# HGRN2 attention and a MetaFormer MLP on one core: the first MLP product by 15 block products for 18, with the attention moved by half a unit

## The chip, the cores and the metric

The kernel runs on one core of a Trainium2 chip. A core has a matrix engine (TensorE, PE in the profile, with its weight loads as PEld), VectorE (DVE), ScalarE (ACT), GpSimd (POOL), and queues that issue DMAs (SP above all). The metric is the device time of one execution in microseconds, the median of several runs. About 1% is what a measurement of this kernel can tell from no change.

## What is computed

A gated linear attention over 4 batches, 8 heads, 768 steps and 48 channels, then layer normalisation and a two-layer MLP with a residual. The reference, cut to what matters:

```python
f = 1.0 / (1.0 + np.exp(-f_logit))
for t in range(S):                       # S = 768, state is 48 x 48 for each batch and head
    state = f[:, :, t, :, None] * state + np.einsum('bhd,bhe->bhde', k[:, :, t], v[:, :, t])
    y[:, :, t] = np.einsum('bhd,bhde->bhe', q[:, :, t], state)
x = y.transpose(0, 2, 1, 3).reshape(B, S, H * D)          # 4 x 768 x 384
xn = (x - mu) / np.sqrt(var + 1e-06) * g_ln
out = x + np.maximum(xn @ w_ch1, 0.0) @ w_ch2             # w_ch1 384 x 1536, w_ch2 1536 x 384
```

Both weight matrices arrive as 64-bit floats; all else is 32-bit.

## The kernel before

**Units.** The 768 steps are cut into 12 units of 64 steps. A unit holds the 64 steps of all four batches, so 256 rows of x, as two groups (g) of 128 rows. For each unit runs an attention and an MLP.

**Attention of unit n**, in named steps: `gates` (transposes of f on TensorE, tile tr, then a sigmoid on ScalarE), `after` and `upto` (running products of the gates by a scan on VectorE, 128 x 1040), `kx` and `k` (transposes of k, then kh = k times after, on VectorE), `q` (transposes of q, qh = q times upto), `kept` (the state scaled), `carried` (the state's share of the result, into py), `scores` (kh by qh, into ps), `causal` (the mask, on VectorE, into sc), `kt` (transposes of kh, tile kp), `values` (sc by v, into py; ScalarE copies it to x), `chunk` (the unit's own state, into pn), `state` (state = kept + pn), `stats` and `norm` (mean and variance, 1/sqrt on POOL, xn on VectorE), `turn` (transposes of xn, tile xp, and on ScalarE the multiplication with the gain, into xt). carried, scores, values and chunk are small products on quarters of the matrix engine, 64 x 64 and 64 x 48.

**MLP of unit n** (`mlp`, a generator: each `yield` ends a step). The first product makes h, 1536 x 256, held transposed as 12 blocks of 128 rows: for each block three matmuls of a 128 x 128 piece of w1 against 256 columns of xt are summed in a PSUM bank (tile ph, line 778), and ScalarE applies the ReLU for two blocks at once (line 780). That is six steps. In blocks of 128 rows of x by 128 of its columns, and 128 by 512 pieces of w1, it is 2 x 3 x 3 = 18 block products. The second product runs from unit 2 on by seven products for eight (tiles pp, line 805; in order p1, p2, p6, p5, p7, p3, p4), from four sums of blocks of h on VectorE (`sums`, tiles s1, s2, s4 and one written over h) and four of w2 (`mix`, tiles mixed1 to mixed4). VectorE and POOL add the results up in p1, p1x, u2x, u4x, u4y, and DMAs write them out. Units 0 and 1 use plain products (tile po, line 786).

**PSUM.** A pool of four single banks (`one_bank`), handed out in turn to tr, kp, xp, ph, po and pp, and a pool of two double banks for py, ps and pn. A tile of the first pool can be written when the fourth tile before it has been read.

**What sets the order.** No scheduler does: two tables of tokens, START for units 0 to 2 and UNIT for each later one, are read from left to right, and each token records the instructions of one step on all engines at once. `a5.norm` is the step norm of unit 5's attention, `m4` the next step of unit 4's MLP, `l6f` the load of f for unit 6, `s4` the sums of unit 4, `f`, `r` and `w` fetch a piece of the weights and turn it into 32 bits, `t` is one third of mix, `d` an idle product that has no use for the result. Each engine takes its instructions in that order. In UNIT before, with m the unit whose MLP runs, all steps of attention n = m + 1 stand between the thirteen steps of MLP m:

```python
a{n}.gates m{m} a{n}.after m{m} m{m} a{n}.upto a{n}.kx a{n}.k m{m} a{n}.q a{n}.kept m{m}
a{n}.kt a{n}.carried a{n}.scores l{o}f l{o}k m{m} a{n}.causal l{o}q s{m} m{m} m{m} a{n}.values
```

Of the kernel before, what the change touches and what calls it, by code (L numbers as in the profile page):

```python
# [302 lines left out]


START = """
l0k f a0.gates a0.kx a0.after l0q l0v l0x d a0.upto f l1f
r d a0.kept a0.k d l1x a0.q l1k a0.carried f l1q a0.scores
a0.causal w a0.kt a0.values a0.stats r w a1.gates a0.norm a0.chunk a0.state a1.after
f a0.turn f a1.upto a1.kx l1v f f f r r m0
a1.k w a1.kept m0 l2k f a1.q f a1.carried a1.kt r a1.scores  # L310
w a1.causal a1.values r l2v r w l2f a1.chunk a1.stats m0 w
m0 f a1.norm r m0 w f a1.turn r w m0 w
r a1.state m1 m1 m1 m1 w l3v r m0 a2.gates m1
m0 r w a2.after l2q m1 w a2.kx a2.k t l3k m0
m0 l2x m0 a2.upto a2.q a2.kept l3q m0 a2.carried a2.scores m1 m1
a2.causal m1 m1 a2.kt a2.values a2.stats a2.norm a2.chunk l3f a2.state m1 m1
a2.turn l4v a3.gates t m2 a3.kx a3.after a3.k m2 a3.upto a3.kept a3.q
m2 a3.carried a3.scores l4k m2 l4q a3.kt l4x m2 m2 l3x l4f
a3.causal s2 a3.values a3.chunk a3.state t m2 m2 a3.stats m2 m2 m2
a3.norm m2 a3.turn m2  # L320
"""
UNIT = """
a{n}.gates m{m} a{n}.after m{m} m{m} a{n}.upto a{n}.kx a{n}.k m{m} a{n}.q a{n}.kept m{m}
a{n}.kt a{n}.carried a{n}.scores l{o}f l{o}k m{m} a{n}.causal l{o}q s{m} m{m} m{m} a{n}.values
a{n}.chunk m{m} a{n}.stats m{m} m{m} l{o}v a{n}.norm m{m} l{o}x a{n}.turn a{n}.state m{m}
"""


# [1 line left out]
def kernel(  # L330
# [19 lines left out]
    nc = tc.nc  # L350
    B, H, S, D = q.shape
    P = 128
    T = 64
    G = B // 2
# [5 lines left out]
    F = moe_w_ch1.shape[1]  # L360
    KD = DM // P
    KF = F // P
    NU = S // T
    W = B * T
    EPS = 1e-6
    LEAST = 1e-12
    PLAIN = 2
    PIECE = 768

    outer = ctx.enter_context(tc.tile_pool(name="outer", bufs=1))  # L370
    ident = outer.tile([P, P], FP32)
    w1 = outer.tile([P, KD, F], FP32)
# [4 lines left out]
    fast = ExitStack()  # L377
    fast.enter_context(tc.manual_schedule())
    consts = fast.enter_context(tc.tile_pool(name="consts", bufs=1))
    raws = fast.enter_context(tc.tile_pool(name="raws", bufs=2))  # L380
    stage = fast.enter_context(tc.tile_pool(name="stage", bufs=2))
# [3 lines left out]
    ps1 = fast.enter_context(tc.tile_pool(name="ps1", bufs=4, space=PSUM))  # L385

    def two_banks(name):
# [152 lines left out]

    pairs = [(g, a) for g in range(G) for a in range(NP)]
    x_of, norm_of, xt_of, h_of, sums_of = {}, {}, {}, {}, {}

    def half(i):
        return slice(64 * i, 64 * i + 64)
# [195 lines left out]
    def turn(n):  # L743
# [8 lines left out]
                              mul=gain[:, m:m + 1])  # L752
        xt_of[n] = xt

    def sums(n):
# [6 lines left out]
        nc.vector.tensor_tensor(out=s1, in0=a21, in1=a22, op=ALU.add)  # L762
        nc.vector.tensor_tensor(out=s2, in0=s1, in1=a11, op=ALU.subtract)
        nc.vector.tensor_tensor(out=a21, in0=a11, in1=a21, op=ALU.subtract)
        nc.vector.tensor_tensor(out=s4, in0=a12, in1=s2, op=ALU.subtract)
        sums_of[n] = s1, s2, a21, s4

    def mlp(n):

        x = x_of.pop(n)  # L770
        xt = xt_of.pop(n)
        h = work.tile([P, KF, W], FP32, tag="h", bufs=2, name=f"h{n}")
        h_of[n] = h
        for i in range(0, KF, 2):
            ph = one_bank(f"ph{n}").rearrange("p (i t) -> p i t", i=2)
            for j in range(2):
                for m in range(KD):
                    nc.tensor.matmul(ph[:, j], lhsT=w1[:, m, (i + j) * P:(i + j + 1) * P],  # L778
                                     rhs=xt[:, m], start=m == 0, stop=m == KD - 1)
            nc.scalar.activation(out=h[:, i:i + 2], in_=ph, func=AF.Relu)  # L780
            yield
        if n < PLAIN:
            for g in range(G):
                po = one_bank(f"po{n}")[:, 0:DM]
                for i in range(KF):
                    nc.tensor.matmul(po, lhsT=h[:, i, g * P:(g + 1) * P], rhs=w2[:, i],  # L786
                                     start=i == 0, stop=i == KF - 1)
# [12 lines left out]
        t1, t2, t3, t4 = mixed  # L800

        def product(name, a, b):
            pp = one_bank(f"p{name}_{n}")[:, 0:CH]
            for i in range(KH):
                nc.tensor.matmul(pp, lhsT=a[:, i], rhs=b[:, i], start=i == 0, stop=i == KH - 1)  # L805
            return pp


        p1, p1x, u2x, u4x, u4y = [xs.tile([P, CH], FP32, tag=name, bufs=1, name=f"{name}_{n}")
                                  for name in ("p1", "p1x", "u2x", "u4x", "u4y")]  # L810

        def add(engine, to, x1, x2, op=ALU.add):
            engine.tensor_tensor(out=to, in0=x1, in1=x2, op=op)  # L813
# [6 lines left out]
        nc.scalar.copy(out=p1, in_=product("p1", a11, b11))  # L820
# [24 lines left out]
        yield  # L845
# [2 lines left out]

    running = {}

    def run(plan):
        for token in plan.split():
            kind, rest = token[0], token[1:]
            if kind == "a":
                n, stage = rest.split(".")
                if int(n) >= NU:
                    continue
                if "a" + n not in running:  # L860
                    running["a" + n] = attention(int(n))
                running["a" + n].pop(stage)()
            elif kind == "m":
                if token not in running:
                    running[token] = mlp(int(rest))
                next(running[token])
            elif kind == "l":
                load(int(rest[:-1]), rest[-1])
            elif kind == "s":
                sums(int(rest))  # L870
            else:
                {"r": read, "w": write, "f": fetch, "t": mix, "d": idle,
                 "T": lambda: mix(nc.gpsimd)}[token]()

    run(START)
    assert not (queue or fetched or opened)
    for m in range(3, NU):
        run(UNIT.format(m=m, n=m + 1, o=m + 2))
        if m == NU - 2:
            worst = consts.tile([P, 1], FP32)  # L880
            nc.vector.tensor_reduce(out=worst, in_=least, axis=mybir.AxisListType.X, op=ALU.min)
# [4 lines left out]
                                    op=ALU.min)  # L886
            nc.vector.tensor_scalar(out=small, in0=least_one, scalar1=LEAST, scalar2=None,
                                    op0=ALU.is_lt)
    fast.close()

    too_small = nc.values_load(small[0:1, 0:1], min_val=0, max_val=1)
# [33 lines left out]
```

## Time and profile before

| | us |
|---|---|
| median of three runs | 487.04 (486.35 to 490.55) |
| the profiled execution | 489.21 |
| its span | 487.5 |
| TensorE busy in it | 466.0 |
| VectorE busy | 258.1 |
| ScalarE busy | 123.1 |
| POOL busy | 61.8 |

The profiled execution is 2.2 us slower than the median, and its span is 1.7 us shorter than its own time. A group's row gives line, engine, operation, out<-in, shapes and count, then busy time and the mean ns of one, then the idle time ahead of it and what ended it. A row of the chain or of the timeline gives start, length, engine and line. Matmuls in float32 are two instructions each; a transpose is one.

### The profile page before, as it was taken

How to read it: one execution, taken by the hardware profiler on the slowest of the kernel's cores; microseconds unless marked ns; L12 is line 12 of the kernel's file. 1: busy time of each engine (PE TensorE's matmuls, PEld its weight loads, DVE VectorE, ACT ScalarE, POOL GpSimd, SP SyncE). 2: the span in 40 equal slices, each digit the busy share in tenths (PEclk: the TensorE clock that was granted, in tenths of full speed). 3: DMA queues.
4: the chain of work that ended last, by engine and by line, in shares of the span. 5: the costliest groups of instructions: out<-in, count | busy, mean ns of one | idle time of the engine just before them, and what ended most of it. 6: DMA issues, size and time to landing. Idle time of an engine off the chain costs nothing.

```text
span 487.5 us, 11965 instructions
## 1 busy us (share of the span) xinstructions
PE 466.0 (96%) x5207; PEld 417.9 (86%) x5207; DVE 258.1 (53%) x388; ACT 123.1 (25%) x253; POOL 61.8 (13%) x90
## 2 busy tenths in 40 slices
PE   5588999999999999999999999999999999999994
PEld 4467886668899999899899899899899899899894
DVE  6799958328175356356355445544644554544031
ACT  3347732013203213212212212222122222222110
POOL 3225431000020020011011002002002002002010
PEclk9998999999999999999999999999999999999999
DMA  9898982324502303503502602512512521200001
GB/s 169 156 249 221 239 202 50 66 50 91 89 11 57 67 10 75 99 11 70 100 11 57 114 11 56 103 21 53 98 27 45 97 40 27 57 3 22 12 9 32
DMA packets 125964, 36.26 MB, mean 74 GB/s; under 512 B 116432, under 2 KB 122064, under 8 KB 125904
## 3 DMA queue, kind: packets, MB, share of 16 engines
q1 hardware_dynamic: 124128, 35.02, 35.1%
q8 instruction: 43, 0.70, 0.6%
q10 hardware_dynamic: 1776, 0.40, 0.4%
q14 instruction: 17, 0.14, 0.1%
HBM read 30.67 MB, written 4.72 MB: 73 GB/s over the span
## 4 chain that ended last, share of the span: by engine, by line
PE 91%; DVE 3%; SPq 3%; DMA 1%; issue 0%; ACT 0%
PE ph L778 38%; PE pp L805 28%; PE po L786 6%; PE tr L568 5%; PE py L686 3%; PE py L646 2%; PE ps L660 2%; SPq L421 2%; PE pn L716 2%; PE kp L676 2%; PE xp L749 1%; DMA w_256words<-in_moe_w_ch_dram 1%; SPq L411 1%; DVE upto L588 0%; DVE xn L739 0%; DVE after L576 0%
## 5 line engine op out<-in xcount | busy, mean ns | idle before, releaser
L778 PE MATMUL ph<-xt,w 128*128 128x256 f32 x864 | 195.5, 381 | 0.0
L778 PEld LDWEIGHTS ph<-xt,w 128*128 128x128 f32 x864 | 161.4, 191 | 21.5 <-ACT xt L751 0.3
L780 ACT ACTIVATE h<-ph 128x512 f32<-128x512 f32 x72 | 42.9, 597 | 168.9 <-PE ph L778 168.9
L805 PE MATMUL pp<-mixed,h 128*128 128x192 f32 x240 | 42.3, 326 | 0.0
L813 POOL TENSOR_TENSOR p1x<-p,x 128x192 f32<-128x192 f32 x10 | 6.3, 631 | 278.2 <-ACT p L820 278.2
L805 PE MATMUL pp<-mixed,s 128*128 128x192 f32 x240 | 41.5, 329 | 0.0
L805 PE MATMUL pp<-w,h 128*128 128x192 f32 x240 | 40.7, 326 | 0.0
L751 ACT ACTIVATE xt<-xp,gain 128x128 f32<-128x128 f32 x72 | 19.9, 376 | 81.5 <-PE xp L749 81.5
L805 PEld LDWEIGHTS pp<-w,h 128*128 128x128 f32 x240 | 39.5, 190 | 0.5
L805 PEld LDWEIGHTS pp<-mixed,s 128*128 128x128 f32 x240 | 38.8, 190 | 0.4
L805 PEld LDWEIGHTS pp<-mixed,h 128*128 128x128 f32 x240 | 39.1, 190 | 0.0
L576 DVE TENSOR_TENSOR_SCAN after<-gates,ends 128x1040 f32<-128x1040 f32 (+1 forms) x13 | 29.3, 2256 | 13.3 <-ACT gates L605 13.3
L664 DVE TENSOR_TENSOR sc<-ps,causal 128x1024 f32<-128x1024 f32 x12 | 14.7, 1224 | 34.1 <-PE ps L660 34.1
L786 PE MATMUL po<-w,h 128*128 128x384 f32 x96 | 32.2, 488 | 0.0
L762 DVE TENSOR_TENSOR s<-h 128x768 f32<-128x768 f32 x10 | 9.6, 958 | 41.2 <-ACT h L780 41.2
L588 DVE TENSOR_TENSOR_SCAN upto<-gates,starts 128x1040 f32<-128x1040 f32 (+1 forms) x13 | 28.1, 2158 | 0.4
L786 PEld LDWEIGHTS po<-w,h 128*128 128x128 f32 x96 | 17.9, 190 | 11.4
L595 DVE TENSOR_TENSOR kh<-tr,after 128x512 f32<-128x512 f32 x24 | 15.4, 683 | 20.6 <-PE tr L568 20.5
L595 DVE TENSOR_TENSOR qh<-tr,upto 128x512 f32<-128x512 f32 x24 | 15.5, 684 | 19.6 <-PE tr L568 19.6
L568 PE MATMUL tr<-ident,fraw 128*128 128x128 f32 x96 | 14.5, 298 | 9.7 <-DMA fraw<-in_f_logit_dram 9.7
L813 DVE TENSOR_TENSOR u2x<-u2x,pp 128x192 f32<-128x192 f32 x20 | 7.1, 354 | 30.7 <-PE pp L805 30.7
L813 DVE TENSOR_TENSOR p<-p,pp 128x192 f32<-128x192 f32 x20 | 7.1, 353 | 30.1 <-PE pp L805 28.6
(112 smaller groups left out, 542.8 us busy)
## 6 DMA issues: line engine op xcount, KB each, us to landing
w_0words<-in_moe_w_ch_dram SPq DMA_DIRECT2D x7, 768.0 KB, 5.3
kraw<-in_k_dram SPq DMA_DIRECT2D x48, 96.0 KB, 3.0
qraw<-in_q_dram SPq DMA_DIRECT2D x48, 96.0 KB, 3.0
v<-in_v_dram SPq DMA_DIRECT2D x48, 96.0 KB, 3.1
fraw<-in_f_logit_dram SPq DMA_DIRECT2D x46, 96.0 KB, 3.0
vx<-in_v_dram SPq DMA_DIRECT2D x48, 48.0 KB, 2.5
out_dram<-p1x SPq DMA_DIRECT2D x19, 48.0 KB, 2.5
out_dram<-u4y SPq DMA_DIRECT2D x19, 48.0 KB, 2.0
```

The costliest lines, as they stand in the source:

```text
L568: nc.tensor.transpose(pt[:, a * P:(a + 1) * P], src[:, g, 2 * a:2 * a + 2].rearrange("p h e -> p (h e)"), ident)
L576: nc.vector.tensor_tensor_scan(out=at["after"].rearrange(flat)[:, c0:c1][:, ::-1], data0=gt[:, c0 + 1:c1 + 1][:, ::-1], data1=ends.rearran ...
L588: nc.vector.tensor_tensor_scan(out=at["upto"].rearrange(flat)[:, c0:c1], data0=gt[:, c0:c1], data1=starts.rearrange(flat)[:, c0:c1], initi ...
L595: nc.vector.tensor_tensor(out=dst[:, segs], in0=pt, in1=by[:, segs, 1:E1], op=ALU.mult)
L664: nc.vector.tensor_tensor(out=new("sc", [P, 2, GA, T]).rearrange("s r e t -> s (r e) t"), in0=at["ps"].rearrange("s r e t -> s (r e) t"), ...
L686: nc.tensor.matmul(py[half(b), r, e * D:(e + 1) * D], lhsT=sc[rows, r, e], rhs=vx[rows, g, a] if r else vt[rows, g, 2 * a], start=n == 0 a ...
L751: nc.scalar.mul(out=xt[:, m, g * P:(g + 1) * P], in_=pt[:, m], mul=gain[:, m:m + 1])
L778: nc.tensor.matmul(ph[:, j], lhsT=w1[:, m, (i + j) * P:(i + j + 1) * P], rhs=xt[:, m], start=m == 0, stop=m == KD - 1)
L780: nc.scalar.activation(out=h[:, i:i + 2], in_=ph, func=AF.Relu)
L786: nc.tensor.matmul(po, lhsT=h[:, i, g * P:(g + 1) * P], rhs=w2[:, i], start=i == 0, stop=i == KF - 1)
L805: nc.tensor.matmul(pp, lhsT=a[:, i], rhs=b[:, i], start=i == 0, stop=i == KH - 1)
L813: engine.tensor_tensor(out=to, in0=x1, in1=x2, op=op)
```

## The change

From unit 3 on the first product is made by 15 block products (`by_blocks`), each of 128 rows of x by 128, or a sum of such blocks, against a 128 x 512 piece of w1, or a sum of such pieces. A product is four matmuls of 128 columns into one PSUM bank. The sums of blocks of x are made for each unit on VectorE (`sums_of_x`, tile y, 128 x 12 x 128), nine instructions. The sums of pieces of w1 (v0 to v13, 128 x 512 each) are made once, in START, by `mix_first`, one instruction at each token `U` (on POOL, twelve) or `u` (on VectorE, one); they take the memory in which the weights were converted.

Five tiles of a bank each (bw, bx, bv, by, bz) are used in a unit. The first product into a bank overwrites it, and a later product adds to what stands there: bx holds the sum of up to six products. After each product the running sum is read: ScalarE copies it to a block of h (the first time) or VectorE adds it to that block or subtracts it, and ScalarE's ReLU follows when a block is complete. The next product into the same bank comes behind that reading.

The tables of the order are written anew. In UNIT the step q of the next attention, kept, kx, k, kt, upto, after and the gates of the one behind it stand in the unit ahead of where they stood, carried and scores follow the third block product, values the fifth, and chunk the last; turn stands between the second product's first two steps. An MLP has 22 steps for 13, and START holds 11 idle products for 3.

The diff, cut to its core:

```diff
 UNIT = """
-a{n}.gates m{m} a{n}.after m{m} m{m} a{n}.upto a{n}.kx a{n}.k m{m} a{n}.q a{n}.kept m{m}
...
+m{m} m{m} m{m} a{n}.carried a{o}.after a{n}.scores a{n}.causal m{m} m{m} a{n}.values m{m} m{m}
...
+    FIRST = 3
...
+    CW = F // 3
+    late = {}
+    def mix_first():
+        changing.close()
+        pool = changing.enter_context(tc.tile_pool(name="late", bufs=1))
...
+        for to, x1, x2, op in ((v[13], b[1, 3], b[2, 3], add), (v[1], v[13], b[1, 2], sub),
...
+            engine = yield
+            engine.tensor_tensor(out=to, in0=x1, in1=x2, op=op)
...
+    def sums_of_x(n):
+        xt = xt_of[n]
+        a = {(g + 1, k + 1): xt[:, k, g * P:(g + 1) * P] for g in range(G) for k in range(KD)}
+        y = late["pool"].tile([P, 12, P], FP32, tag="y", name=f"y{n}")
...
+                (nc.vector, wide[:, 4 * P:6 * P], flat[:, W:2 * W], flat[:, 0:W], sub),
...
+            engine.tensor_tensor(out=to, in0=x1, in1=x2, op=op)
...
+    def by_blocks(n, h):
+        a, y = y_of.pop(n)
+        v, b = late["v"], late["b"]
+        KB = CW // P
...
+        def product(bank, left, right):
+            new = bank not in banks
+            if new:
+                banks[bank] = one_bank(f"{bank}_{n}").rearrange("p (i t) -> p i t", t=P)
+            for i in range(KB):
+                nc.tensor.matmul(banks[bank][:, i], lhsT=right[:, i * P:(i + 1) * P], rhs=left,
+                                 start=new and i == 0, stop=True, skip_group_check=True)
+            return banks[bank]
+        def copy(to, bank, scale=1.0):
+            nc.scalar.activation(out=out[to], in_=bank, func=AF.Copy, scale=scale)
+        def add(to, bank, op=ALU.add):
+            nc.vector.tensor_tensor(out=out[to], in0=out[to], in1=bank, op=op)
+        def relu(to, bank=None):
+            nc.scalar.activation(out=out[to], in_=out[to] if bank is None else bank, func=AF.Relu)
+        copy((1, 3), product("bw", y[12], b[2, 3]))
+        yield
+        copy((2, 3), product("bx", y[11], v[11]))
+        yield
+        copy((1, 1), product("bv", y[3], b[2, 1]))
+        yield
+        add((1, 3), product("bx", y[9], b[3, 3]))
+        yield
+        add((1, 1), product("by", y[4], b[1, 1]))
+        yield
+        add((1, 1), product("bx", a[1, 3], v[7]), ALU.subtract)
+        relu((1, 1))
+        yield
+        add((1, 3), product("by", a[1, 1], v[13]), ALU.subtract)
+        relu((1, 3))
+        yield
+        copy((1, 2), product("bx", y[10], v[10]))
+        yield
+        add((1, 2), product("by", y[1], v[1]), ALU.subtract)
+        yield
+        copy((2, 2), product("bz", a[2, 2], v[0]), -1.0)
+        yield
+        add((2, 2), product("bx", y[2], b[3, 2]), ALU.subtract)
+        yield
+        add((2, 2), product("by", y[14], b[1, 2]))
+        relu((2, 2))
+        yield
+        add((1, 2), product("bz", y[6], b[2, 2]))
+        relu((1, 2))
+        yield
+        relu((2, 1), product("bx", y[8], v[8]))
+        yield
+        bank = product("by", y[5], v[5])
+        nc.vector.tensor_tensor(out=out[2, 3], in0=bank, in1=out[2, 3], op=ALU.subtract)
+        relu((2, 3))
+        yield
...
-        for i in range(0, KF, 2):
...
+        if n < FIRST:
+            for i in range(0, KF, 2):
...
+        else:
+            yield from by_blocks(n, h)
```

The fifteen products are numbered 1 to 15 in this order; add 6 is the reading of product 6 by VectorE, copy 8 that of product 8 by ScalarE.

More of the change, by code (lines that the diff above doesn't have):

```diff
@@ L305 @@
 START = """
[L306 to L320, printed above, removed]
+l0k f l0q a0.gates l0x a0.after l0v f r a0.kx a0.upto l1f
+d a0.kept a0.k d l1x d d a0.q l1k a0.carried d a0.scores
+d a0.causal a0.values w d r a0.kt a0.stats f l1q d a1.gates
@@ new lines @@
+f l1v a0.chunk d w a0.norm a1.after a0.state a0.turn d a1.upto a1.kx
+a1.k d f r w m0 a1.kept m0 a1.q f f r
+w a1.carried a1.kt r f r l2k f a1.scores a1.causal f l2v
+w l2f f a1.values r a1.chunk f a1.stats m0 m0 r w
+a1.norm m0 a1.turn r w r w a1.state m0 m1 m1 m1
+w m1 w a2.gates r m0 m1 m0 a2.after r l2x w
+l2q w a2.kx a2.k a2.upto m1 m0 a2.q m0 m0 l3q l3k
+a2.kept l3v m0 a2.carried a2.scores U m1 a2.causal a2.values m1 a2.stats a2.norm
+m1 m1 U l3f a2.kt U m1 a2.turn m1 a3.gates T a2.chunk
@@ L321 @@
+m2 a3.after a2.state a3.kx l3x l4f m2 a3.k a3.upto a3.kept m2 a3.q
+U m2 U l4q a3.carried a3.scores a3.kt U U a3.causal U l4x
+a4.gates l4k a3.values T l4v U U a3.chunk m2 a3.stats a3.state t
+l5v U a3.norm m2 s2 a4.after m2 l5f a3.turn m2 m2 a4.kx
+a4.k a4.upto l5x l5k m2 U u m2 a4.q m2 y3 l5q
+a5.gates a4.kt m2 l6f a4.kept
 """
 UNIT = """
-a{n}.gates m{m} a{n}.after m{m} m{m} a{n}.upto a{n}.kx a{n}.k m{m} a{n}.q a{n}.kept m{m}
-a{n}.kt a{n}.carried a{n}.scores l{o}f l{o}k m{m} a{n}.causal l{o}q s{m} m{m} m{m} a{n}.values
@@ L325 @@
-a{n}.chunk m{m} a{n}.stats m{m} m{m} l{o}v a{n}.norm m{m} l{o}x a{n}.turn a{n}.state m{m}
+m{m} m{m} m{m} a{n}.carried a{o}.after a{n}.scores a{n}.causal m{m} m{m} a{n}.values m{m} m{m}
+m{m} m{m} a{n}.stats m{m} m{m} m{m} a{n}.norm m{m} m{m} m{m} s{m} a{n}.chunk
+m{m} a{n}.turn m{m} a{o}.upto a{p}.gates a{o}.kx l{p}v a{o}.k a{n}.state m{m} m{m} m{m}
+a{o}.kt y{n} m{m} a{o}.q l{p}q l{p}x a{o}.kept l{p}k m{m} l{z}f
 """
@@ L385 @@
     ps1 = fast.enter_context(tc.tile_pool(name="ps1", bufs=4, space=PSUM))
+    changing = ExitStack()
+    stage = changing.enter_context(tc.tile_pool(name="stage", bufs=2))
     def two_banks(name):
@@ L539, in mix, with mix_step @@
             engine.tensor_tensor(out=to, in0=x1, in1=x2, op=ALU.subtract)
+    CW = F // 3
[3 more added lines that the diff above has]
+        pool = changing.enter_context(tc.tile_pool(name="late", bufs=1))
+        late["pool"] = pool
+        v = {i: pool.tile([P, CW], FP32, tag=f"v{i}", name=f"v{i}")
+             for i in (0, 1, 5, 7, 8, 10, 11, 13)}
+        late["v"] = v
+        b = {(k, j): w1[:, k - 1, (j - 1) * CW:j * CW] for k in (1, 2, 3) for j in (1, 2, 3)}
+        late["b"] = b
+        add, sub = ALU.add, ALU.subtract
+        for to, x1, x2, op in ((v[13], b[1, 3], b[2, 3], add), (v[1], v[13], b[1, 2], sub),
+                               (v[8], b[3, 1], b[3, 2], add), (v[10], b[2, 1], v[8], sub),
+                               (v[8], b[1, 1], v[8], add), (v[0], v[1], b[2, 2], sub),
+                               (v[0], v[0], v[10], sub), (v[5], b[1, 2], b[1, 3], sub),
+                               (v[5], v[5], b[3, 3], sub), (v[7], b[2, 1], b[3, 1], sub),
+                               (v[7], v[7], b[3, 3], sub), (v[11], b[1, 1], b[3, 3], add)):
+            engine = yield
+            engine.tensor_tensor(out=to, in0=x1, in1=x2, op=op)
+        yield
+        nc.vector.scalar_tensor_tensor(out=v[13], in0=b[1, 1], scalar=-1.0, in1=v[13],
+                                       op0=ALU.mult, op1=sub)
+        yield
+    def mix_step(engine=nc.vector):
+        if "steps" not in late:
+            late["steps"] = mix_first()
+            next(late["steps"])
+        late["steps"].send(engine)
     pairs = [(g, a) for g in range(G) for a in range(NP)]
-    x_of, norm_of, xt_of, h_of, sums_of = {}, {}, {}, {}, {}
+    x_of, norm_of, xt_of, y_of, h_of, sums_of = {}, {}, {}, {}, {}, {}
     def half(i):
@@ L753, in turn @@
         xt_of[n] = xt
+    def sums_of_x(n):
+        xt = xt_of[n]
+        a = {(g + 1, k + 1): xt[:, k, g * P:(g + 1) * P] for g in range(G) for k in range(KD)}
+        y = late["pool"].tile([P, 12, P], FP32, tag="y", name=f"y{n}")
+        at = {p: y[:, i] for i, p in enumerate((14, 6, 3, 8, 12, 5, 11, 9, 4, 10, 1, 2))}
+        y_of[n] = a, at
+        wide = y.rearrange("p i t -> p (i t)")
+        flat = xt.rearrange("p k t -> p (k t)")
+        add, sub = ALU.add, ALU.subtract
+        for engine, to, x1, x2, op in (
+                (nc.vector, wide[:, 4 * P:6 * P], flat[:, W:2 * W], flat[:, 0:W], sub),
+                (nc.vector, wide[:, 2 * P:4 * P], flat[:, W:2 * W], flat[:, 2 * W:3 * W], add),
+                (nc.vector, at[11], a[2, 1], at[8], sub), (nc.vector, at[9], a[1, 3], at[11], sub),
+                (nc.vector, at[4], a[1, 1], at[11], add), (nc.vector, at[10], a[2, 2], a[1, 3], sub),
+                (nc.vector, at[1], a[1, 1], a[2, 2], add), (nc.vector, at[2], at[10], at[8], sub),
+                (nc.vector, y[:, 0:2], xt[:, 0:2, 0:P], xt[:, 0:2, P:W], add)):
+            engine.tensor_tensor(out=to, in0=x1, in1=x2, op=op)
     def sums(n):
@@ L766, in sums @@
         sums_of[n] = s1, s2, a21, s4
+    def by_blocks(n, h):
+        a, y = y_of.pop(n)
+        v, b = late["v"], late["b"]
+        KB = CW // P
+        out = {(g, j): h[:, (j - 1) * KB:j * KB, (g - 1) * P:g * P] for g in (1, 2)
+               for j in (1, 2, 3)}
+        banks = {}
+        def product(bank, left, right):
[43 more added lines that the diff above has]
+        relu((2, 1), product("bx", y[8], v[8]))
+        yield
+        bank = product("by", y[5], v[5])
+        nc.vector.tensor_tensor(out=out[2, 3], in0=bank, in1=out[2, 3], op=ALU.subtract)
+        relu((2, 3))
+        yield
     def mlp(n):
@@ L773, in mlp @@
         h_of[n] = h
-        for i in range(0, KF, 2):
[L775 to L781, printed above, removed]
+        if n < FIRST:
+            for i in range(0, KF, 2):
+                ph = one_bank(f"ph{n}").rearrange("p (i t) -> p i t", i=2)
+                for j in range(2):
+                    for m in range(KD):
+                        nc.tensor.matmul(ph[:, j], lhsT=w1[:, m, (i + j) * P:(i + j + 1) * P],
+                                         rhs=xt[:, m], start=m == 0, stop=m == KD - 1)
+                nc.scalar.activation(out=h[:, i:i + 2], in_=ph, func=AF.Relu)
+                yield
+        else:
+            yield from by_blocks(n, h)
         if n < PLAIN:
@@ L870, in run @@
                 sums(int(rest))
+            elif kind == "y":
+                if FIRST <= int(rest) < NU:
+                    sums_of_x(int(rest))
             else:
                 {"r": read, "w": write, "f": fetch, "t": mix, "d": idle,
-                 "T": lambda: mix(nc.gpsimd)}[token]()
+                 "T": lambda: mix(nc.gpsimd), "u": mix_step,
+                 "U": lambda: mix_step(nc.gpsimd)}[token]()
     run(START)
@@ L877 @@
     for m in range(3, NU):
-        run(UNIT.format(m=m, n=m + 1, o=m + 2))
+        run(UNIT.format(m=m, n=m + 1, o=m + 2, p=m + 3, z=m + 4))
         if m == NU - 2:
@@ L888 @@
                                     op0=ALU.is_lt)
+    changing.close()
     fast.close()
```

1 line of the change is left out of this document (removed).

## The prediction

> **What bounds the kernel now.** I read the busy times of the page first, then the chain of waits, then the windows, then the chain in order of time over one unit.
>
> ```profile
> PE 466.0 (96%) x5207; PEld 417.9 (86%) x5207; DVE 258.1 (53%) x388; ACT 123.1 (25%) x253; POOL 61.8 (13%) x90
> PE ph L778 38%; PE pp L805 28%; PE po L786 6%; PE tr L568 5%; PE py L686 3%; PE py L646 2%; PE ps L660 2%; SPq L421 2%; PE pn L716 2%; PE kp L676 2%; PE xp L749 1%; DMA w_256words<-in_moe_w_ch_dram 1%; SPq L411 1%; DVE upto L588 0%; DVE xn L739 0%; DVE after L576 0%
> ```
>
> TensorE is busy 96% of the span, and the largest share of the chain, 38%, is line 778, the product that is replaced. The windows (us; busy time of PE, PEld, DVE, ACT, POOL; granted clock; DMA) tell where PE is not busy:
>
> ```profile
> 0.00:40.00 40.00, 26.93 (x420) 21.75 (x420) 31.88 (x48) 17.45 (x30) 11.02 (x20) 0.96 0.96 197
> 40.00:80.00 40.00, 38.44 (x290) 32.26 (x291) 31.69 (x36) 21.95 (x36) 18.31 (x11) 0.96 0.71 179
> 80.00:120.00 40.00, 39.97 (x406) 28.07 (x405) 20.99 (x34) 5.76 (x14) 0.92 (x2) 1.00 0.38 72
> ...
> 160.00:200.00 40.00, 40.00 (x464) 37.16 (x463) 19.50 (x30) 8.64 (x20) 3.25 (x6) 1.00 0.33 62
> ```
>
> 13.1 us are idle in the first 40 us, 1.6 in the next, none in the middle. So a unit lasts as long as PE's own work in it. The chain over one unit (start, length, what):
>
> ```profile
> 162.88 2.59 PE ph L778 x12
> 165.48 0.87 PE kp L676 x8
> 166.35 1.08 PE py L646 x64
> 167.43 0.95 PE ps L660 x64
> 168.38 2.79 PE ph L778 x12
> 171.16 3.90 PE pp L805 x24
> 175.06 1.08 PE py L686 x64
> 176.14 0.93 PE pn L716 x64
> 177.07 8.00 PE pp L805 x48
> 185.07 0.66 PE xp L749 x6
> 185.73 1.95 PE pp L805 x12
> 187.68 0.87 PE tr L568 x8
> 188.55 7.77 PE ph L778 x36
> 196.32 0.87 PE tr L568 x8
> 197.20 2.59 PE ph L778 x12
> 199.79 0.87 PE tr L568 x8
> ```
>
> The pieces join without a gap: 199.79 + 0.87 - 162.88 = 37.78 us a unit. The reader should see the paces. 12 ph instructions (6 matmuls, each of two instructions) of 256 columns take 2.59 us, 216 ns each; 12 pp of 192 columns 1.95 us, 163 each; 8 kp or tr of 128 columns 0.87 us, 109 each. Time follows the columns, 0.84 ns each and some 2 ns. A switch from small tiles back to full ones costs 0.20 us (2.79 for 2.59; 8.00 for 4 x 1.95), and the switch into them about 0.13 (py 1.08 beside pn 0.93, which follows small tiles).
>
> **The new product's pace.** Per unit 36 matmuls of 256 columns go (72 instructions, 6 x 2.59 = 15.54 us). 15 x 4 matmuls of 128 columns come: 120 instructions, each with its own weights. The columns fall by a sixth (72 x 256 to 120 x 128), but the weight loads rise from 72 to 120. Equal time would need 15.54 / 120 = 129.5 ns an instruction. No row has such a matmul at 128 columns: kp, tr and xp are transposes, whose loads are shorter. What joins the two is a tr followed by a ph:
>
> ```profile
> 200.17 0.49 PE L568 MATMUL tr<-ident,qraw 128*128 128x128 f32 x3
> 200.28 0.14 PEld L568 LDWEIGHTS tr<-ident,qraw 128*128 128x128 f32 x1
> 200.39 0.52 PEld L778 LDWEIGHTS ph<-xt,w 128*128 128x128 f32 x3
> 200.50 0.60 PE L778 MATMUL ph<-xt,w 128*128 128x256 f32 x2
> L778 PEld LDWEIGHTS ph<-xt,w 128*128 128x128 f32 x864 | 161.4, 191 | 21.5 <-ACT xt L751 0.3
> ```
>
> The load of the first ph starts at 200.39 and its matmul at 200.50, 0.11 us later, though the load is recorded with 191 ns: the matmul need not wait for the record's end. So a full load fits behind a 128-column matmul. Bounds: 109 ns (the transposes' pace) and 191 (the record's whole length). I take 109, because this row shows the very pair: 120 x 0.109 = 13.08 us, 2.46 less than 15.54.
>
> The Trainium skill ("TensorE: Matmul & The Clock Gate", Back-to-back issue gap) says that a stream of load-matmul pairs is spaced by both operations, and gives 81 ns for 128 columns where the matmul alone would take 56. By that ratio, an estimate from the page, 109 would be some 158 ns and the product 18.9 us, slower than before. The pair above speaks against it; a run of such pairs is not in this trace.
>
> **The moved attention.** On PE, unit 5's first product ended around the scores of unit 6 before:
>
> ```order
> L778 MATMUL ph5_2380<-xt5_2273,w1_59 128x256 x6
> L676 MATMUL kp6_2389<-ident_58,kh6_2353 128x128 x4
> L676 MATMUL kp6_2395<-ident_58,kh6_2353 128x128 x4
> L646 MATMUL py6_2401<-kept6_2378,qh6_2364 64x48 x32
> L660 MATMUL ps6_2434<-qh6_2364,kh6_2353 64x64 x32
> L778 MATMUL ph5_2475<-xt5_2273,w1_59 128x256 x6
> L805 MATMUL pp1_5_2501<-w2_60,h5_2314 128x192 x6
> ```
>
> Now it begins there, and the transposes of q, k and the gates stand in the unit before:
>
> ```order
> L935 MATMUL pp4_4_2532<-mixed4_124,h4_2122 128x192 x6
> L844 MATMUL bw_5_2547<-y5_2483,w1_59 128x128 x4
> L844 MATMUL bx_5_2553<-y5_2483,v11_1030 128x128 x4
> L844 MATMUL bv_5_2559<-y5_2483,w1_59 128x128 x4
> L689 MATMUL py6_2565<-kept6_2526,qh6_2503 64x48 x32
> L703 MATMUL ps6_2599<-qh6_2503,kh6_2436 64x64 x32
> L844 MATMUL bx_5_2553<-y5_2483,w1_59 128x128 x4
> L844 MATMUL by_5_2639<-y5_2483,w1_59 128x128 x4
> ```
>
> The unit has three visits to small tiles for two (values and chunk are parted): +0.33 us. PE's bare sum is 37.78 - 15.54 + 13.08 + 0.33 = 35.65 us. START gets five groups more of 0.87 us (f, k, kt, q of unit 4, f of unit 5), which units 9 and 10 lose: nothing in sum. The loads go with their steps on SP, each at least half a unit ahead, and the middle window shows DMA at 0.33: nothing.
>
> **The new waits.** Behind values come ten products on two alternating banks and bz; each goes into a bank that VectorE or ScalarE must have read:
>
> ```order
> L844 MATMUL bx_5_2553<-xt5_2378,v7_1027 128x128 x4
> L844 MATMUL by_5_2639<-xt5_2378,v13_1031 128x128 x4
> L844 MATMUL bx_5_2553<-y5_2483,v10_1029 128x128 x4
> L844 MATMUL by_5_2639<-y5_2483,v1_1025 128x128 x4
> L844 MATMUL bz_5_2711<-xt5_2378,v0_1024 128x128 x4
> L844 MATMUL bx_5_2553<-y5_2483,w1_59 128x128 x4
> L844 MATMUL by_5_2639<-y5_2483,w1_59 128x128 x4
> L844 MATMUL bz_5_2711<-y5_2483,w1_59 128x128 x4
> L844 MATMUL bx_5_2553<-y5_2483,v8_1028 128x128 x4
> L844 MATMUL by_5_2639<-y5_2483,v5_1026 128x128 x4
> L759 MATMUL pn6_2755<-v6_2007,kt6_2470 64x48 x32
> L935 MATMUL pp1_5_2793<-w2_60,h5_2546 128x192 x6
> ```
>
> Before, ph and pp stood there, each in a buffer read long ago. VectorE's queue at this place, where s1 followed the causal product at once before, is now:
>
> ```order
> L707 TENSOR_TENSOR sc6_2632<-ps6_2599,causal_105 128x1024
> L852 TENSOR_TENSOR h5_2546<-h5_2546,bx_5_2553 128x4x128
> L852 TENSOR_TENSOR h5_2546<-h5_2546,by_5_2639 128x4x128
> L852 TENSOR_TENSOR h5_2546<-h5_2546,bx_5_2553 128x4x128
> L852 TENSOR_TENSOR h5_2546<-h5_2546,by_5_2639 128x4x128 x2
> L745 BN_STATS stats6_2702<-x6_2677 128x6
> ```
>
> So nine adds of 128x512 out of PSUM stand between causal and s1, with statistics and normalisation among them. Their prices:
>
> ```profile
> L595 DVE TENSOR_TENSOR qh<-tr,upto 128x512 f32<-128x512 f32 x24 | 15.5, 684 | 19.6 <-PE tr L568 19.6
> L664 DVE TENSOR_TENSOR sc<-ps,causal 128x1024 f32<-128x1024 f32 x12 | 14.7, 1224 | 34.1 <-PE ps L660 34.1
> L702 DVE BATCH_NORM_STATS2 stats<-x 128x6 f32<-128x384 f32 x24 | 13.0, 540 | 4.6 <-ACT x L693 4.5
> L703 DVE BATCH_NORM_AGGREGATE mv<-stats 128x2 f32<-128x6 f32 x24 | 4.4, 182 | 0.8
> L539 DVE TENSOR_TENSOR mixed<-w 128x384 f32<-128x384 f32 x6 | 3.3, 550 | 0.0
> L762 DVE TENSOR_TENSOR s<-h 128x768 f32<-128x768 f32 x10 | 9.6, 958 | 41.2 <-ACT h L780 41.2
> L764 DVE TENSOR_TENSOR h<-h x10: 949/1347/1347, 135.9 to 470.1; 128x768 f32<-128x768 f32 x10
> 211.37 0.64 POOL L813 TENSOR_TENSOR p1x<-p,x 128x192 f32<-128x192 f32 x1 [28.02 <-ACT p L820]
> 221.47 0.86 DVE L739 TENSOR_SCALAR xn<-x,mv,rstd 128x384 f32<-128x384 f32 x2
> L780 ACT ACTIVATE h<-ph 128x512 f32<-128x512 f32 x72 | 42.9, 597 | 168.9 <-PE ph L778 168.9
> ```
>
> An add is like qh, 0.69 us; its ends are 0.64 (two thirds of the 958 row) and 1.35 (the h<-h row, in place). Copies and ReLUs are like h<-ph, 0.60. I lay the queues out from the end of the scores (0), with 0.2 us from a product's last issue to its reader and 0.04 between engines, the first from the three tr above (0.49 us to the end of the last, 0.16 more than 3 x 0.109), the second my estimate for a handover.
>
> - PE: products 4 and 5, switch included, to 1.98; values to 3.16; 6 (bx) to 4.27; 7 (by) to 5.15.
> - DVE: causal to 1.37, adds 4 and 5 to 2.06 and 2.87, add 6 4.47 to 5.16, add 7 to 6.04. Product 8 starts at 5.20, 9 at 6.08: no wait worth naming.
> - ACT: ReLU 1,1 and 1,3 to 6.68, then copy 8 to 7.28. Add 9 waits for that copy: 7.32 to 8.01. Statistics (two of 0.54 and two of 0.18) to 9.44; adds 11 and 12 to 10.82; xn to 11.68; add 13 to 12.37; add 15 to 13.06.
> - PE goes on with 9 to 15 and ends them at 12.24; chunk to 13.3. The first pp takes the buffer of bx, whose last ReLU follows that of block 1,2 on ACT: 13.0, 13.6. It starts at 13.64 where 13.3 was due: 0.3 us of wait.
> - s1 and s2 end near 16; pp of s2 comes at 19.6. y (three sums of 256 columns, six of 128) is by the 550 and 958 rows some 0.42 and 0.29 us each, 3.0 in all; it ends two products ahead of its use.
>
> VectorE's load rises by 9 x 0.69 + 3.0 = 9.2 us a unit, from 19.5 in 40 us to some 29 in 36: covered, with 1 us of slack ahead of causal. Unit: 35.65 + 0.3 + 0.2 for what such joints lose = 36.15, 1.63 less. Bounds: no wait, 35.65; all nine adds at 1.35, below.
>
> The 1.35 us of h<-h stand where POOL adds p1x; the shortest took 0.95. The Trainium skill ("SBUF — State Buffer", SBUF: two separate sides) says that a VectorE instruction with two SBUF inputs and a GpSimd one that reads SBUF exclude each other; the trace agrees (949 and 1347 ns). By that rule the PSUM adds escape and y pays at most 0.6 us once a unit, within the slack: the sum stays.
>
> **Both ends.** The last unit, and the idle products:
>
> ```profile
> 452.00 15.54 PE ph L778 x72
> 467.54 13.66 PE pp L805 x84
> L530 PE MATMUL idle<-nothing 128*128 128x256 f32 x6 | 2.8, 634 | 0.0
> ```
>
> The last unit stands alone: 13.08 + 13.66 + 0.5 (ReLU ahead of the first pp) = 27.25 for 29.20, 1.95 less. The idle products rise from 3 to 11; eight at 2.8 / 3 = 0.93 us are 7.5 us if nothing hides them, but the cover is the 13.1 us of idle time at the start, and a clock held up there could give back 0.04 x 80 = 3.2 us. I take 0, ends -3 and +7.5. The weight sums (12 on POOL) stand behind 80 us, where POOL is busy 0.92 us in 40: nothing, unless a normalisation stands behind them.
>
> **The sum.** Eight units (3 to 10) x 1.63 = 13.0, the last 1.95: 15.0 us. The profiled execution took 489.21 (span 487.5): 474.2. The median, 487.04, lies 2.2 lower: 472.0. My bare case is 467 (no waits, some gain at the start); with every joint 0.5 us worse it is 476.
>
> **The rivals.**
> - Slower: an add in place costs 1.35. VectorE then has 7 x 1.35 + 2.3 = 11.8 us between values and s1 where PE has ten products, 8.7: 3.1 + 0.3 of wait, unit 39.05, +1.27 x 8 - 1 = 496. It decides at (2.13 - 0.3) / 7 above 0.69, about 0.95 us an add. For it: the h<-h row; against: its 949 ns case. 0.12.
> - Weights bind: a pace of 150 ns, halfway to the record, gives 18.0 us, unit 40.57, and with the last unit +25: 512. It decides at about 127 ns with the switch. Against it the 0.11 us pair; the page named above is for it. 0.06.
> - Nothing won: handovers and idle products take it back, 1.2 us of wait a unit (9.6 us) and +4 at the start: 485. VectorE at 80% speaks for it, the layout against. 0.13.
> - All covered, clock gained: 467. 0.07.
>
> **The numbers.** The forecast has 0.62, at 472 (own range 467 to 477). The range 466 to 486 leaves out the first two rivals, 0.18. About 1% is what a measurement of this kernel can tell from no change: under 482.2 lie the forecast, the covered case and a quarter of the third rival, 0.72; 0.10 lie within, 0.18 above.
>
> **What would show it.** Right: a product of 8 instructions in about 0.87 us; adds near 0.69; units of some 36.1; a short PE wait on ACT ahead of the first pp. Wrong: products at 1.0 us or more (loads), PE waits on h adds above 2 us a unit (VectorE), an idle start longer than 15 us.

## The result, and the profile after

The changed kernel took 474.65 us (median of 4 runs, 472.82 to 475.21) beside 487.59 us for the kernel before (median of 4 runs, 486.35 to 490.55): a ratio of 0.972, 95% interval 0.9667 to 0.9772. The forecast was 472.0, with 466 to 486 as the range. The profiled execution took 472.82 us, its span 470.7.

The page's first part and its chain by lines:

```profile
PE 452.5 (96%) x5655; PEld 420.3 (89%) x5655; DVE 332.3 (71%) x543; ACT 149.7 (32%) x298; POOL 93.9 (20%) x110
PE pp L935 29%; PE bx L844 11%; PE ph L906 9%; PE by L844 9%; PE po L916 7%; PE tr L611 6%; PE bz L844 3%; PE py L729 3%; PE py L689 3%; PE ps L703 2%; PE pn L759 2%; PE kp L719 2%; SPq L428 2%; PE bv L844 2%; PE bw L844 2%; PE xp L792 2%
```

TensorE is still what a unit waits for, at the same 96%; VectorE went from 53% to 71% without becoming the bound. The 38% that line 778 had are now 9% of ph (units 0 to 2) and 27% of the five banks. The chain over the unit whose first block product starts at 224.94 (start, length, what):

```profile
224.94 0.89 PE bw L844 x8
225.83 0.89 PE bx L844 x8
226.72 0.89 PE bv L844 x8
227.62 1.08 PE py L689 x64
228.69 0.95 PE ps L703 x64
229.64 1.09 PE bx L844 x8
230.73 0.89 PE by L844 x8
231.62 1.08 PE py L729 x64
232.70 1.09 PE bx L844 x8
233.79 0.89 PE by L844 x8
234.68 1.04 PE bx L844 x8
...
241.98 1.08 PE pn L759 x64
243.06 2.15 PE pp L935 x12
...
259.11 1.95 PE pp L935 x12
261.07 0.89 PE bw L844 x8
```

From bw to bw it is 36.13 us, where 37.78 were before. A product of eight instructions takes 0.89 us, 111.6 ns an instruction. The first product after a visit to small tiles takes 1.09, the first pp 2.15: 0.20 more, as predicted. The eighth product (234.68) takes 1.04: it starts 0.15 us late, because add 6 must have read bx. Behind pn the first pp starts without a wait.

VectorE's new instructions, by form:

```profile
L852 DVE TENSOR_TENSOR h<-h,by 128x512 f32<-128x512 f32 x36 | 24.8, 688 | 16.9 <-PE by L844 15.9
L852 DVE TENSOR_TENSOR h<-h,bx 128x512 f32<-128x512 f32 x27 | 18.3, 679 | 15.9 <-PE bx L844 15.9
L814 DVE TENSOR_TENSOR y<-xt 128x256 f32<-128x256 f32 x27 | 10.6, 419 | 0.0
L814 DVE TENSOR_TENSOR y<-xt,y 128x128 f32<-128x128 f32 x27 | 7.1, 289 | 0.6
```

An add in place costs what qh cost (684 ns), not what h<-h cost. What the units gave: eight times 1.65 is 13.2 us. The last unit, alone from 437.10 to 464.60, took 27.5 us for 29.2. That makes 14.9 us.

### The profile page after: what moved, and what is told of

It is laid out like the page before. It is cut to its first block, busy times and chain, and to the rows that moved or that the text cites. A ratio compares the mean times of both kernels' runs of the same rounds, so it can differ in the third digit from the quotient of the medians.

```text
span 470.7 us, 13070 instructions
## 1 busy us (share of the span) xinstructions
PE 452.5 (96%) x5655; PEld 420.3 (89%) x5655; DVE 332.3 (71%) x543; ACT 149.7 (32%) x298; POOL 93.9 (20%) x110
## 4 chain that ended last, share of the span: by engine, by line
PE 90%; DVE 3%; SPq 3%; DMA 1%; issue 0%; ACT 0%
PE pp L935 29%; PE bx L844 11%; PE ph L906 9%; PE by L844 9%; PE po L916 7%; PE tr L611 6%; PE bz L844 3%; PE py L729 3%; PE py L689 3%; PE ps L703 2%; PE pn L759 2%; PE kp L719 2%; SPq L428 2%; PE bv L844 2%; PE bw L844 2%; PE xp L792 2%
## 5 line engine op out<-in xcount | busy, mean ns | idle before, releaser
L906 PE MATMUL ph<-xt,w 128*128 128x256 f32 x216 | 48.6, 381 | 0.5 <-DVE kh L638 0.5
L906 PEld LDWEIGHTS ph<-xt,w 128*128 128x128 f32 x216 | 40.4, 190 | 6.5 <-issue 0.9
L855 ACT ACTIVATE h<-h 128x512 f32<-128x512 f32 x45 | 28.3, 630 | 38.5 <-DVE h L852 37.2
L852 DVE TENSOR_TENSOR h<-h,by 128x512 f32<-128x512 f32 x36 | 24.8, 688 | 16.9 <-PE by L844 15.9
L721 ACT COPY kt<-kp 128x512 f32<-128x512 f32 x24 | 12.9, 591 | 57.5 <-PE kp L719 57.5
L852 DVE TENSOR_TENSOR h<-h,bx 128x512 f32<-128x512 f32 x27 | 18.3, 679 | 15.9 <-PE bx L844 15.9
L844 PE MATMUL bx<-y,v 128*128 128x128 f32 x216 | 29.4, 279 | 0.0
L736 ACT COPY x<-py 128x384 f32<-128x384 f32 x24 | 10.3, 483 | 59.0 <-PE py L729 59.0
L844 PEld LDWEIGHTS bx<-y,v 128*128 128x128 f32 x216 | 26.2, 192 | 0.7
L943 POOL TENSOR_TENSOR p1x<-p,x 128x192 f32<-128x192 f32 x10 | 10.3, 1032 | 70.9 <-ACT p L950 70.9
```

What stands on the lines that cost most here:

```text
L844: nc.tensor.matmul(banks[bank][:, i], lhsT=right[:, i * P:(i + 1) * P], rhs=left, start=new and i == 0, stop=True, skip_group_check=True)
L852: nc.vector.tensor_tensor(out=out[to], in0=out[to], in1=bank, op=op)
L855: nc.scalar.activation(out=out[to], in_=out[to] if bank is None else bank, func=AF.Relu)
```

## Experiments

Each is the changed kernel with one edit, timed beside the kernel before. "A" is the theory that the gain is TensorE's time in the product.

**The changed kernel once more**, for the runs beside it.

> The changed kernel once more, unaltered, so that the small edits beside it are compared on the same chip: 474.7 us (473 to 475.5) by every theory.

474.65 us (473.75 to 477.26, 6 runs) beside 488.78 us (11 runs): ratio 0.9714, 0.969 to 0.9738.

**The new order with the old product.**

```diff
-    FIRST = 3
+    FIRST = S // T
...
                 nc.scalar.activation(out=h[:, i:i + 2], in_=ph, func=AF.Relu)
                 yield
+                if n > 2:
+                    for _ in range((1, 1, 2, 2, 2, 1)[i // 2]):
+                        yield
```

> The new order with the old first product: all units use the plain product, its six steps placed among the fifteen places of the new table; the sums of w1 are still made, y isn't. Theory A (the gain is TensorE's time in the product; the moved attention only gives the cover): a unit is 37.78 us plus 0.33 for the third visit to small tiles, 38.1, and the start keeps its 1.6 us: 487.6 + 2.6 - 1.6 = 488.6 us, 486 to 491. Rival B (the new order brings the gain by itself): 474 to 479. The first product takes 15.5 us a unit again in both.

492.32 us (491.97 to 493.63), ratio 1.0074, 1.0046 to 1.0102: not faster, and if anything slower, by under 1%. The scores of one unit and the next stand 38.12 us apart in its trace, the 38.1 of theory A. So the moved attention wins nothing by itself; rival B falls. The time is 3.7 us above the expectation and 1.3 beyond its end: the 1.6 us that I had booked to the start after one profile is not a property of the order (below), and the kernel before stood at 488.8 here, 1.2 above the base of that sum. The two leave 0.9 us open.

**What sets the pace of a product.** Each product as eight matmuls of 64 columns:

```diff
-                nc.tensor.matmul(banks[bank][:, i], lhsT=right[:, i * P:(i + 1) * P], rhs=left,
-                                 start=new and i == 0, stop=True, skip_group_check=True)
+                for t in (0, 64):
+                    nc.tensor.matmul(banks[bank][:, i, t:t + 64],
+                                     lhsT=right[:, i * P:(i + 1) * P], rhs=left[:, t:t + 64],
+                                     start=new and i == 0 and t == 0, stop=True,
+                                     skip_group_check=True)
```

> Each product as eight matmuls of 64 columns, each with its own weights: twice the loads for the same columns. Theory A (a load of 128 columns needs 107 to 111 ns too, so that 128 columns cover it with nothing to spare): 16 instructions of 107 to 111 ns, 1.71 to 1.78 us a product, 0.85 x 15 x 9 = +115 us: 590 us (580 to 600). Rival (loads run far ahead, and the columns alone set the pace): 0.89 to 0.95 us a product, 475 to 484.

593.95 us in one run. Its chain:

```profile
207.55 1.79 PE bx L845 x16
209.34 1.79 PE bv L845 x16
211.12 1.08 PE py L689 x64
...
215.08 1.79 PE by L845 x16
```

Sixteen instructions of 64 columns take 1.79 us, 111.8 ns each: the same as with 128 columns. Half the columns buy nothing, so at 128 columns it is no longer the columns that set the pace: they alone would need 109 ns, and an instruction takes 111.6. That the weight load sets it fits the transposes, which have the same columns but shorter loads (recorded with 141 ns for 192) and keep to 109. A run that changes the loads and neither columns nor the number of instructions was not made.

And the opposite, 512 columns behind one load, operands exchanged:

```diff
-            for i in range(KB):
-                nc.tensor.matmul(banks[bank][:, i], lhsT=right[:, i * P:(i + 1) * P], rhs=left,
-                                 start=new and i == 0, stop=True, skip_group_check=True)
+            nc.tensor.matmul(banks[bank], lhsT=left, rhs=right, start=new, stop=True,
+                             skip_group_check=True)
```

> Operands exchanged in the fifteen products: the block of x is the stationary side and 512 columns of w1 move, one matmul for four, so 30 weight loads a unit for 120. The blocks of h come out transposed, which changes what the second product gets; all other instructions are the same. Theory A (the loads hide behind the 128 columns but for 2 ns each): a product falls from 0.893 to 2 x 0.429 = 0.858 us, 0.53 us a unit, 470 us (468.5 to 471.5). Rival C (part of the 111 ns is load time that 107 ns of columns don't cover): products well below 0.85, or a gain beyond 8 us: under 467.

469.78 us (468.89 to 470.65), ratio 0.9631, 0.9599 to 0.9663. In its chain a product is two instructions:

```profile
230.21 0.86 PE by L843 x2
231.07 1.08 PE py L729 x64
232.15 1.05 PE bx L843 x2
```

0.86 for 0.89 us, and units of 35.65. So 120 instructions with their loads, instead of 30, cost 0.5 us a unit. The kernel can't have it: the blocks come out with x's rows on the partitions, and the second product wants the features there.

**The price of an add.** A second VectorE instruction out of the same bank behind eight of the nine adds, its result unused; 192 columns (0.36 us) in the one, 512 (0.70 us) in the other:

```diff
             nc.vector.tensor_tensor(out=out[to], in0=out[to], in1=bank, op=op)
+            nc.vector.tensor_tensor(out=late["spare"][:, 0:2, 0:96], in0=out[to][:, 0:2, 0:96],
+                                    in1=bank[:, 0:2, 0:96], op=op)
```

> A second VectorE instruction of 128x192 out of the same bank behind each of eight adds (0.35 us), its result unused: an add costs 1.04 us. By the laid-out queues the banks come free later: products 8, 9, 14 and 15 wait, ScalarE's last ReLUs come later, and the first pp starts 1.1 us later in each unit: 474.7 + 8 x 1.1 + 1 = 484.5 us (481 to 488). Rival (VectorE, busy some three quarters of a unit, has slack that hides 2.8 us more): 475 to 477.

484.49 us (483.4 to 487.96, 10 runs), ratio 0.9926, 0.9901 to 0.9952. Units 37.15. Its chain shows where the 1.02 us went:

```profile
240.32 1.10 PE bx L845 x8
241.42 0.02 issue
241.45 0.70 DVE h L853
242.15 0.02 issue
242.17 0.36 DVE spare L854
242.53 0.04 issue
242.58 1.16 PE bx L845 x8
243.74 0.99 PE by L845 x8
...
248.30 1.15 PE bx L845 x8
249.44 0.02 issue
249.47 1.16 PE by L845 x8
```

The sixth product (bx), its add, the second instruction, and only then the eighth product, 2.26 us after the sixth began, where it is 1.98 in the changed kernel: 0.28 us. Products 8 and 9 take another 0.2 (2.15 us for 1.94), and products 14 and 15, which now wait as well, 0.55 (2.33 for 1.78). So a product waits for the reader of its bank, as the prediction laid it out.

> The same with a second instruction of 128x512: an add costs 1.37 us, the price of the rival in the prediction. The queues laid out give 3.8 us more a unit: 474.7 + 8 x 3.8 + 3 = 508 us (500 to 514), slower than the kernel before. The prediction's shorter sum gave 496. If VectorE has slack: below 485.

499.86 us in one run, units of mostly 38.88: slower than the kernel before, as the prediction's first rival had it (496, units of 39.05), but less than this expectation. VectorE's spare time in a unit hides this only in part: eight times 0.36 us (2.9) cost 1.02 us a unit, eight times 0.70 (5.6) cost 2.75. Between the two, the new product would lose its gain (37.78) at about 1.16 us an add.

**The idle products.** Eleven back to three:

```diff
-d a0.kept a0.k d l1x d d a0.q l1k a0.carried d a0.scores
+d a0.kept a0.k d l1x d  a0.q l1k a0.carried  a0.scores
...
```

> The changed kernel with 3 idle products instead of 11. Theory A (the start gained 1.6 us because the idle products hold the clock up): a stretch of half clock returns between 40 and 55 us, 476.3 us (475.5 to 477.5). Rival (the idle products are in the way): the eight cost up to 4.7 us of TensorE, so 470 to 473.5. Neither: 474.7.

475.03 us (473.62 to 478.27), ratio 0.9729, 0.9698 to 0.976: neither. The windows of this kernel, columns as before:

```profile
0.00:40.00 40.00, 26.78 (x340) 22.00 (x344) 30.10 (x46) 15.81 (x27) 10.93 (x19) 0.83 0.90 184
40.00:80.00 40.00, 38.65 (x382) 32.61 (x374) 32.63 (x41) 23.17 (x39) 19.07 (x12) 1.00 0.72 188
```

The granted clock of the first 40 us is 0.83, where the two profiles with eleven idle products have 0.96 and 0.91. But TensorE is busy in only 26.78 of these 40 us, and the time doesn't move. The eight idle products show neither help nor harm.

**Fewer visits to small tiles.** chunk behind values, and turn where chunk was:

```diff
-m{m} m{m} m{m} a{n}.carried a{o}.after a{n}.scores a{n}.causal m{m} m{m} a{n}.values m{m} m{m}
-m{m} m{m} a{n}.stats m{m} m{m} m{m} a{n}.norm m{m} m{m} m{m} s{m} a{n}.chunk
-m{m} a{n}.turn m{m} a{o}.upto a{p}.gates a{o}.kx l{p}v a{o}.k a{n}.state m{m} m{m} m{m}
+m{m} m{m} m{m} a{n}.carried a{o}.after a{n}.scores a{n}.causal m{m} m{m} a{n}.values a{n}.chunk m{m} m{m}
+m{m} m{m} a{n}.stats m{m} m{m} m{m} a{n}.norm m{m} m{m} m{m} s{m} a{n}.turn
+m{m} m{m} a{o}.upto a{p}.gates a{o}.kx l{p}v a{o}.k a{n}.state m{m} m{m} m{m}
```

> chunk directly behind values, so that a unit has two visits to the small tiles, and turn ahead of the second product's first step, so that its 0.66 us stand where chunk covered the last ReLUs. Theory A (each visit costs 0.33 us, and the first pp needs the ReLU of block 1,2): 0.33 - 0.07 = 0.26 us a unit won, 472.6 us (471.8 to 473.6). Rival (chunk's cover is missed: the first pp waits 0.4 us or more for ScalarE): 475 to 477.

478.04 us (477.09 to 479.23), ratio 0.9784, 0.976 to 0.9808: 3.4 us (0.7%) slower than the changed kernel beside it, and the two intervals do not meet, so the proposed 0.26 us a unit is not won. Quiet units stayed at 36.13 us. The list of waits (engine, line, what it waited for: us in total, times, longest) and the chain show two losses:

```profile
PEld pp L935 <- ACT h L855: 2.6, 8, 0.3
```

```profile
163.00 0.93 PE pn L759 x64
163.94 1.06 issue
165.00 1.05 PE bx L844 x8
```

The load of the first pp waits 0.3 us in each unit for the ReLU of bx, which takes back what the joined visit gave. The timeline of a quiet unit tells why it waits here and not in the changed kernel:

```profile
247.71 0.82 PE L792 MATMUL xp<-ident,xn 128*128 128x128 f32 x6
247.98 0.58 ACT L855 ACTIVATE h<-bx 128x512 f32<-128x512 f32 x1
248.61 3.55 PEld L935 LDWEIGHTS pp<-w,h 128*128 128x128 f32 x22 [0.32 <-ACT h L855]
```

The transposes of xn run while bx is still to be read, so their two tiles are in other banks; what is left for the first pp is the bank of bx. In the changed kernel, where turn stands behind the first pp, that pp has another bank (below). So it is turn's new place, and not the lost cover of chunk, that brings the wait. Chunk behind values with turn left where it was is an order that was not run, and for it the 0.26 us stay open. Besides, there are two holes of 1.06 us, one of them the row at 163.94, in which TensorE waited for nothing that the profile shows. In this profile they are 2.1 us.

A second try put the next gates' transposes ahead of the first pp too:

```diff
-m{m} m{m} a{n}.stats m{m} m{m} m{m} a{n}.norm m{m} m{m} m{m} s{m} a{n}.turn
-m{m} m{m} a{o}.upto a{p}.gates a{o}.kx l{p}v a{o}.k a{n}.state m{m} m{m} m{m}
+m{m} m{m} a{n}.stats m{m} m{m} m{m} a{n}.norm m{m} m{m} m{m} s{m} a{n}.turn a{p}.gates
+m{m} m{m} a{o}.upto a{o}.kx l{p}v a{o}.k a{n}.state m{m} m{m} m{m}
```

> As the kernel with chunk behind values, with the transposes of the next gates also ahead of the second product's first step, so that 0.87 us more stand between the last product and the first pp. Theory (that kernel's units stayed at 36.13 us because the first pp waited 0.25 us for the last ReLU of bx and then showed its weight load; its other 3 us are holes of 1.06 us in which TensorE waits for nothing, behind the now joined small tiles): a quiet unit is 35.8 us, the holes stay, 475 us (473 to 477). Rival (the joined small tiles cost time in every unit): units of 36.1 or more, 477 to 479.

480.99 us (479.37 to 481.91), ratio 0.9856, 0.9821 to 0.989: worse again, with no unit of 35.8 while two attentions run: 36.74 at best. Its list of waits:

```profile
PEld tr L611 <- ACT h L855: 1.9, 6, 0.3
PE pp L935 <- ACT xt L794: 2.3, 6, 0.4
PE bx L844 <- issue: 1.3, 1, 1.3
```

Now the gates' transposes wait 0.3 us for the ReLU of bx, and the first pp 0.4 us for ScalarE to read xp, whose bank it takes, behind the ReLUs. So neither of my two forecasts for this place held: the wait that I removed came back on the next instruction of ScalarE's queue. Of the three orders tried, that of the change is the fastest.

**The kernel before once more**, for its start.

> The kernel before once more, for a second profile of its start: units of 37.78 us again by every theory. If the start of one and the same kernel varies (the changed kernel's first product of unit 3 began at 152.5 and at 157.1 us in two profiles), unit 4's scores end some us off the place in the first profile; if it doesn't vary for this kernel, within 0.5 us.

492.82 us in one run, span 491.1; its units are again 37.78. The row that stood at 149.90 in the first profile:

```profile
152.95 0.87 PE tr L568 x8
```

So the start of one kernel varies by 3 us between two executions. The changed kernel's first block product began at 152.68 and, unaltered, at

```profile
157.24 0.89 PE bw L844 x8
```

Less the five groups moved into the start (4.35 us), that is 148.3 and 152.9, beside 149.9 and 152.95 before: no difference that these four profiles show.

## Why the prediction was right

The direction and the size held, and so did the main mechanism: the gain is TensorE's time in the product. The median came 2.65 us above the forecast, inside the range. One step, the wait ahead of the first pp, was wrong, and a pace taken too short made up for it.

- **The pace.** 109 ns was taken, 111.6 measured: 0.31 us a unit more. The step's reading, that a full load fits behind a 128-column matmul, was off by those 2.6 ns: by the run with 64 columns it is most likely the load that sets the pace, just not at a price that matters. The weights rival was then right about who binds and wrong about the length. The ratio drawn from the Trainium skill ("TensorE: Matmul & The Clock Gate", Back-to-back issue gap), 158 ns, does not hold for these float32 products, though its statement that both operations set the spacing does.
- **The visits.** 0.33 us for the third one: units of the new order with the old product grew from 37.78 to 38.12.
- **The waits.** 0.3 us were put ahead of the first pp, because it was to take the bank of bx. None stands there, and the sign that was named, a short wait of PE on ACT, did not come. The bank is another one: in the last unit the first pp starts while ScalarE still reads bx.

```profile
450.44 0.58 ACT L855 ACTIVATE h<-bx 128x512 f32<-128x512 f32 x1
450.77 2.44 PE L935 MATMUL pp<-w,h 128*128 128x192 f32 x14
```

  In the built program the first pp has the bank of bv in every unit, and that was read 10 us and more before. The four banks are not handed out strictly in turn: one that is held over several products, as those of bx and by are, is passed over, and the rule of the fourth tile before holds only while every tile is read soon. Instead, 0.15 us stand ahead of product 8, where the laid-out queue had 0.05. The queue was also quicker than laid out. The ReLU of bx ended 13.0 us after the scores (206.54) for 13.6. Half of this was there at add 6, which started 4.2 us after the scores (233.83) for 4.5: its product was 0.1 us early, and the add came 0.04 us behind it for 0.2. The rest came further on, where the records of successive instructions overlap by some 0.1 us, on VectorE as on ScalarE, and I had laid them end to end:

```profile
205.43 0.63 ACT L855 ACTIVATE h<-h 128x512 f32<-128x512 f32 x1 [0.75 <-DVE h L852]
205.96 0.58 ACT L855 ACTIVATE h<-bx 128x512 f32<-128x512 f32 x1
```

- **A unit.** 36.15 predicted, 36.13 measured, and part of that agreement is luck. The bare 35.65 with 0.31 for the pace and 0.15 for product 8 are 36.11. The pace was 0.31 too low, and the 0.5 for waits and joints some 0.3 too high.
- **VectorE.** An add at 0.69: 0.68 to 0.69. y at 3.0 us: 2.55 by the timeline (219.86 to 222.41), since its instructions of 419 and 289 ns overlap too. Some 29 us in 36: 27 (26.94 and 27.81 in two units); the prediction had added a unit's 9.2 us to the 19.5 of a window of 40 us, and by a unit's share of that (18.4) it is 27.6. The rival of the dear add fell with the row of 688 ns. Its mechanism is real, as the doubled add shows, but its point of decision lies at about 1.16 us, not 0.95. That was a slip in the sum: seven adds of 0.69 and the 2.3 us are 7.1, and TensorE has 8.7 us of products there, so the first 1.6 us cost nothing. With them the prediction's own sum gives 1.18.
- **Both ends.** Last unit 27.25 predicted, 27.5 measured: here too the 0.5 us for a ReLU ahead of the first pp are not there, and the fifteen products took 13.83 us for 13.08. Start 0: no difference found.
- **The base.** The sum gave 474.2 from the profiled execution, and I took off 2.2 us because that execution lay above the median of three. Later medians of the kernel before, over 11 and 13 runs, were 488.8 and 487.9, so most of this subtraction was not due. The 15.0 us that were forecast, and the 14.9 of the units in the profile, stand beside 12.9 in the first comparison and 14.1 in the second. The 0.9 to 2.1 us between them are not explained; the start of an execution alone moves by 3 to 5 us.

## What to carry to other kernels

Before fewer multiplications are traded for narrower matmuls, find the pace of one instruction at the new width: here the gain of a sixth of the columns held because an instruction of 128 columns takes no longer than one of 64 (111.6 and 111.8 ns) and hardly longer than its columns, and at 64 it would have been lost several times over. Sums that stay in PSUM put a reader between two products of one bank, so other TensorE work should stand between them: here one product of 0.89 us was 0.15 us short for a reader of 0.69 (product 8), and two were enough, until the reader took 1.05 (products 14 and 15). And where tiles are held for long, look up which bank the next tile gets: its wait can move with the order, as it did when turn was moved. And when a profile's start differs by a few us, take a second profile of the same kernel before giving that a cause.

## What was not expected

A weight load recorded with 188 to 192 ns repeats every 112 ns: its record is longer than its pace. The holes of 0.8 to 1.3 us at or after the joined small tiles came in both kernels that joined them, two in each profile, and not in the changed kernel. In the 3 us around the one at 163.94 the DMA queues show (packets, MB, share)

```profile
q8 instruction: 1, 0.02, 2.7%
```

a packet of instructions; values and chunk issue 128 matmuls and as many loads in 2 us there. That the instructions came too late is a guess that no run here tested, and the kernel before, which also joined them, shows no such hole.
